# A fused attention and two expert layers on one core: conversions that keep a word in PSUM, pieces of 768 columns, one more shared buffer

## The chip, the core and the metric

The kernel runs on one core of a Trainium2 chip. The metric is the device time of one execution in microseconds, lower is better. The engines are TensorE (PE; its weight loads are listed as PEld), VectorE (DVE), ScalarE (ACT) and GpSimd (POOL). SyncE (SP) issues the DMA transfers.

## What is computed

```python
def _attn_ref(q, k, v, centroids):              # q, k, v: (2, 8, 768, 64)
    q_assign = np.argmax(np.einsum('bhsd,hcd->bhsc', q_n, c_n), axis=-1)
    k_assign = np.argmax(np.einsum('bhsd,hcd->bhsc', k_n, c_n), axis=-1)
...
    scores = np.where(mask, scale * q @ k.T, -1000000000.0)
    attn = np.exp(scores - np.max(scores, axis=-1, keepdims=True))
    attn = attn / (np.sum(attn, axis=-1, keepdims=True) + 1e-09)
    return np.matmul(attn, v)
...
def _moe_ref(x, w_in, w_out):                   # 1536 tokens, 512 -> 2048 -> 512
    h = x @ w_in
    return (h * np.cos(h)) @ w_out
...
def _moe2_ref(x, w_in, w_out):
    h = x @ w_in
    return (h * (1.0 / (1.0 + np.exp(-h)))) @ w_out
```

The code is condensed. A query sees only the keys of its own cluster (16 clusters for each head). The attention's result, 1536 tokens of 512 numbers, goes through the first expert layer and then the second. The four weight matrices come in with eight bytes for each number.

## The kernel before

**Numbers.** A product that must keep the accuracy of 32 bits is made of three passes of TensorE on 16-bit halves: high by high, high by low, low by high. So nearly every operand is split: a high half is a cast (mostly on ScalarE), a low half is the value less its high half (VectorE or GpSimd).

**Weights.** `conv` (L683) turns 512 columns of double-width numbers, loaded into a staging buffer, into 32-bit floats by integer operations on VectorE: L692 shifts the upper word and writes the target, L694 takes the sign and exponent from the upper word and joins them with what L692 wrote, in place, and the low word follows in one of two ways. Either VectorE joins it (L701), or, where the table `LOW` says so (2 of every 4), ScalarE makes a number of it (L698) and GpSimd adds it (L699). There are 64 such conversions: 16 for each of the two matrices of layer 1 (`w1_prep`, L782), 16 for the second matrix of layer 2 (`w2_convert`, L853; its result goes to DRAM and returns later), and 16 for the first matrix of layer 2 (`layer2`, L1101), after the attention's buffers have been given up. Then the weights are scaled and split: high half on ScalarE (L738) or GpSimd (L739), low half on VectorE (L750), on GpSimd, or by TensorE (`pe_lo`, L722).

**Attention** (L869). Seven units of one or two tiles of 128 queries, eight heads each: 96 tiles of 128 queries by 768 keys. Of each: scores on TensorE into a PSUM buffer (L890), the row maximum on VectorE (L900), scale and bias of the exponent (L904, L905; VectorE or GpSimd), the exponential on ScalarE into one of four buffers `e` (L919), the high half on ScalarE (L926) or VectorE (L928), the low half on GpSimd (L933) or VectorE (L935), a transposing DMA into a buffer of kind `pT` (L512), and the product with v on TensorE (L943). After eight heads VectorE makes x from the sums (L952 to L954, L960) and splits it (L967, L969, or ScalarE and GpSimd, L970), and a DMA transposes it.

**Layers.** `layer1_in` (L996) takes a unit's x through the first matrix in pieces of `EW` columns: TensorE into PSUM (L1019 to L1021), then L1034 (ScalarE), L1035 (VectorE), a sine (L1037), L1040 (VectorE), the high half (L1042, ScalarE) and the low half (L1043, GpSimd). `layer1_out` (L1049) makes the second product. `layer2` does the same in three passes of 512 tokens, once layer 1 is done: L1170 and L1172 split x, then pieces of `EW` columns (L1190 to L1206) and the second product (L1221 to L1223).

**Buffers.** PSUM has three tiles `pb` of 1024 columns, which hold scores, pieces of the layers, transposes on TensorE and the sums of the preparation, and two tiles of 512 (`g2_ps`, `xn_ps`). In SBUF there are four buffers `e` of `EW` columns and `NGEN` shared buffers `gen` of 768 columns, which serve four kinds; `LEAST` says how many are kept back for each kind (`pT` 3).

**What sets the order.** Each step is a task with a duration, a priority, its predecessors and the buffers that it takes. When the program is built, a list scheduler (`Graph.run`, L139) goes through the tasks in a model of time and takes on each engine the ready task of lowest priority number whose buffers are free; some tasks may go to either of two engines (`alt`), with a bias from the table. The priorities are sums of the entries of the table `T` (L22). What comes out is a fixed order for each engine. `port=True` marks tasks of VectorE that the model does not let run beside GpSimd.

Of the kernel before, what the change touches and what calls it, by code (L numbers as in the profile page):

```python
# [10 lines left out]
I32 = mybir.dt.int32  # L11
# [7 lines left out]
FG = 2.0 ** -19  # L19


T = dict(PW_IN=-2428, PW_OUT=-477, PW_STEP=783, W_AHEAD=-382, KV0=-981, KSTEP0=-32964, V0=33297, Q0=262, KSTEP=-17295,  # L22
         PREP=-1180, PREPQ=1313, LD=4990, LOB=-0.03, WB=-2.09, HB=1.22, EB=0.63, KB=-13.72, GB=2.92, CB=2.75, XB=1.77,
         SB=0.5, L2B=0.5, PV=-1944, HI=1053, LO=13021, XP=-1707, G1=1614, GE=-20317, GC=-1920, G2=1781, GO=-4433,
         W2=5268, XD=-9186, TB=2, WH=50.28, GATE=0)
UNITS = [(0, 0, 1), (0, 1, 1), (0, 2, 2), (0, 4, 2), (1, 0, 2), (1, 2, 2), (1, 4, 2)]

LOW = (2,2,2,2)

PRE = ((0,0),(1,0),(1,1),(0,1,0,1))  # L30

# [7 lines left out]

GRAM_XN = ()  # L40

EW = 1024
NE = 4
NGEN = 11

LEAST = {'stg':2,'natk':2,'ph':4,'pT':3}

WX, WXC = (0, 1), (1, 3)
EXP_BITS = 0x7F800000
# [185 lines left out]
def dve(cols, fast=False):  # L235
    return 0.069 + cols / (1920 if fast else 960)
# [10 lines left out]
def pool2(cols):  # L247
    return 0.15 + cols * 0.001887
# [21 lines left out]
def fused_kernel(tc, q, k, v, cent, w1i, w1o, w2i, w2o, out, dbg=None):  # L270
# [4 lines left out]
    P = 128  # L275
# [24 lines left out]
    with tc.manual_schedule(), tc.tile_pool(name="dram", bufs=1, space=DRAM) as dpool:  # L300
# [379 lines left out]
            xs_task[b] = add("DVE", 0.3, f, [sready[b, hp] for hp in range(NPAIR)], u * 1000)  # L680


        def conv(dst, acc, src, shape3, pri, dst_buf=None, pool=None, deps=(), dst_deps=(), add_low=False):  # L683

            w = Buf(pool or p_ws)
            wa = lambda: l2["ws"][w.ap] if isinstance(w.ap, int) else w.ap
            wi = lambda: wa().rearrange("p (a b) -> p a b", a=shape3) if shape3 else wa()
            word = lambda z: wa().rearrange("p (c two) -> p c two", two=2)[:, :, z]
            d = lambda: dst().bitcast(I32)
            l = add("SP", dma(P * WC * 8), lambda: SP.dma_start(out=wi(), in_=src), deps, pri - T["W_AHEAD"], acq=[w], lat=LLAT)  # L690
            ex = [dst_buf] if dst_buf else []
            a = add("DVE", dve(WC, True), lambda: DV.tensor_scalar(  # L692
                d(), word(1), 3, 0x3FFFFFFF, op0=ALU.logical_shift_left, op1=ALU.bitwise_and), [l, *dst_deps], pri, acq=ex, use=[w], port=True)
            b_ = add("DVE", dve(WC), lambda: DV.scalar_tensor_tensor(  # L694
                d(), word(1), -0x40000000, d(), op0=ALU.bitwise_and, op1=ALU.bitwise_or), [a], pri - 1, use=[w, *ex], port=True)
# [86 lines left out]
        def w1_prep():  # L782
# [41 lines left out]
            for d in range(ND):  # L824
# [276 lines left out]
        def layer2(l1_last):  # L1101
# [204 lines left out]
```

## Time and profile before

| | us |
|---|---|
| median of 3 executions | 826.79 (824.79 to 829.62) |
| the profiled execution | 824.2 |
| its span, from the first to the last instruction | 822.5 |
| TensorE busy, matmuls | 715.3 (87% of the span) |
| VectorE busy | 541.2 (66%) |
| ScalarE busy | 490.8 (60%) |
| GpSimd busy | 230.9 (28%) |
| mean granted TensorE clock | 0.958 of full speed |

The shares are means over the whole span, and the stages differ: the second expert layer, some 255 us at the end, has hardly any transfers and no GpSimd work, while the preparation of the weights and the attention lie in the first 460 us. A stage is therefore read by itself, in a table of windows, and the order of the work within it from a timeline of one engine. "Busy" leaves out waiting. The idle time in front of an instruction is put down to what ended it.

### The profile page before, as it was taken

How to read it: one execution, taken by the hardware profiler on the slowest of the kernel's cores; microseconds unless marked ns; L12 is line 12 of the kernel's file. 1: busy time of each engine (PE TensorE's matmuls, PEld its weight loads, DVE VectorE, ACT ScalarE, POOL GpSimd, SP SyncE). 2: the span in 40 equal slices, each digit the busy share in tenths (PEclk: the TensorE clock that was granted, in tenths of full speed). 3: DMA queues.
4: the chain of work that ended last, by engine and by line, in shares of the span. 5: the costliest groups of instructions: out<-in, count | busy, mean ns of one | idle time of the engine just before them, and what ended most of it. 6: DMA issues, size and time to landing. Idle time of an engine off the chain costs nothing.

```text
span 822.5 us, 16553 instructions
## 1 busy us (share of the span) xinstructions
PE 715.3 (87%) x6744; PEld 487.2 (59%) x6744; DVE 541.2 (66%) x1094; ACT 490.8 (60%) x702; POOL 230.9 (28%) x197
## 2 busy tenths in 40 slices
PE   2486677988779887899999999995999999999998
PEld 1353346777668765787787788882444444444443
DVE  7889988888789788989779756668670044004400
ACT  3769787888867766779659655548770045004400
POOL 3321634265452355346337323330000000000000
PEclk9967898999998999999999999997999999999999
DMA  8925799899999979978977986442312000000000
GB/s 273 358 71 160 196 196 189 148 167 187 177 183 195 248 146 174 176 194 176 183 163 127 214 183 216 141 132 75 104 51 77 26 1 0 26 26 1 0 26 26
DMA packets 233900, 111.27 MB, mean 135 GB/s; under 512 B 199520, under 2 KB 221536, under 8 KB 233824
## 3 DMA queue, kind: packets, MB, share of 16 engines
q1 hardware_dynamic: 233824, 110.23, 60.7%
q8 instruction: 52, 0.85, 0.4%
q14 instruction: 24, 0.20, 0.1%
HBM read 50.36 MB, written 10.49 MB: 74 GB/s over the span
## 4 chain that ended last, share of the span: by engine, by line
PE 58%; DVE 14%; DMA 13%; ACT 5%; issue 5%; POOL 2%; SPq 2%; POOLq 0%; DVEq 0%; ACTq 0%
DMA gen<-gen 7%; PE pb L1191 5%; PE pb L1192 5%; PE pb L1190 5%; PE pb L1019 4%; PE pb L1021 4%; PE pb L1020 4%; PE xn_ps L943 3%; PE pb L890 3%; DVE small L900 3%; PE xn_ps L1221 3%; PE g_ps L1221 3%; PE xn_ps L1223 3%; PE xn_ps L1222 3%; PE g_ps L1222 3%
## 5 line engine op out<-in xcount | busy, mean ns | idle before, releaser
L933 POOL TENSOR_TENSOR gen<-e,gen 128x768 f16<-128x768 f32 x67 | 110.0, 1656 | 63.4 <-ACT gen L926 47.3
L1078 PE MATMUL g_ps<-gT,w 128*128 128x256 f16 (+1 forms) x448 | 111.1, 260 | 3.3 <-POOL gT L1043 3.3
L919 ACT ACTIVATE e<-pb,small 128x768 f32<-128x768 f32 x96 | 94.7, 990 | 31.3 <-DVE small L905 11.9
L1019 PE MATMUL pb<-xT,w 128*128 128x256 f16 (+1 forms) x448 | 111.3, 260 | 1.8 <-DMA xT<-e 1.6
L1077 PE MATMUL g_ps<-gT,w 128*128 128x256 f16 (+1 forms) x448 | 111.2, 260 | 0.9 <-ACT x2s L1084 0.9
L1020 PE MATMUL pb<-xT,w 128*128 128x256 f16 (+1 forms) x448 | 111.2, 260 | 0.0
L1021 PE MATMUL pb<-xT,w 128*128 128x256 f16 (+1 forms) x448 | 111.2, 260 | 0.0
L1079 PE MATMUL g_ps<-gT,w 128*128 128x256 f16 (+1 forms) x448 | 111.2, 260 | 0.0
L900 DVE TENSOR_REDUCE small<-pb 128x1 f32<-128x768 f32 x96 | 89.3, 950 | 19.0 <-PE pb L890 17.0
L1202 DVE SCALAR_TENSOR_TENSOR e<-e,pb 128x1024 f32<-128x1024 f32 x24 | 29.3, 1219 | 105.2 <-ACT e L1200 105.1
L890 PE MATMUL pb<-kst,qst 96*128 96x512 f16 (+3 forms) x384 | 80.2, 343 | 18.0 <-ACT e L919 9.7
L943 PE MATMUL xn_ps<-vst,gen 128*128 128x64 f16 x1728 | 68.5, 196 | 21.5 <-DMA gen<-gen 19.8
L943 PEld LDWEIGHTS <-gen 128*128 128x128 f16 x1728 | 63.1, 100 | 33.5 <-DMA gen<-gen 26.4
L1190 PE MATMUL pb<-x2T,w 128*128 128x512 f16 x192 | 73.7, 384 | 4.5 <-ACT x2T L1170 4.5
L1043 POOL TENSOR_TENSOR gT<-e,gT 128x1024 f16<-128x1024 f32 x24 | 52.2, 2176 | 89.3 <-ACT gT L1042 80.4
L1191 PE MATMUL pb<-x2T,w 128*128 128x512 f16 x192 | 73.7, 384 | 2.5 <-DVE x2T L1172 2.5
L1192 PE MATMUL pb<-x2T,w 128*128 128x512 f16 x192 | 73.6, 383 | 0.0
L926 ACT ACTIVATE gen<-e 128x768 f16<-128x768 f32 x87 | 70.4, 840 | 2.1 <-DMA gen<-gen 0.9
L890 PEld LDWEIGHTS <-qst 128*128 128x128 f16 (+1 forms) x384 | 37.1, 101 | 41.7 <-issue 23.1
L1077 PEld LDWEIGHTS <-w 128*128 128x128 f16 x448 | 44.2, 99 | 9.8 <-issue 2.2
L1079 PEld LDWEIGHTS <-w 128*128 128x128 f16 x448 | 44.2, 99 | 7.8 <-issue 3.9
L1019 PEld LDWEIGHTS <-w 128*128 128x128 f16 x448 | 44.5, 99 | 5.6 <-DMA xT<-e 1.8
(201 smaller groups left out, 1515.0 us busy)
## 6 DMA issues: line engine op xcount, KB each, us to landing
ws<-in_moe_w_out_dram SPq DMA_DIRECT2D x24, 512.0 KB, 4.3
gT<-in_moe_w_in_dram SPq DMA_DIRECT2D x16, 512.0 KB, 5.7
ws<-in_moe_w_in_dram SPq DMA_DIRECT2D x16, 512.0 KB, 3.9
xT<-in_moe_w_out_dram SPq DMA_DIRECT2D x8, 512.0 KB, 4.8
w_dram<-x2s SPq DMA_DIRECT2D x16, 256.0 KB, 3.0
st<-w_dram SPq DMA_DIRECT2D x8, 512.0 KB, 4.4
gen<-in_k_dram SPq DMA_DIRECT2D x8, 384.0 KB, 6.7
gen<-in_v_dram SPq DMA_DIRECT2D x8, 384.0 KB, 5.2
```

The source lines that it names most:

```text
L890: PE.matmul(out=sbk.ap[:, c0:c1], lhsT=qs.ap[:kk, a, h], rhs=kb.ap[:kk, a, j].rearrange("p t c -> p (t c)")[:, c0:c1], start=(a == 1), sto ...
L900: DV.tensor_reduce(out=sm.ap[:, 0:1], in_=sbk.ap[:, :S], axis=AX.X, op=ALU.max, negate=True)
L943: PE.matmul(out=o, lhsT=hb.ap[:, pi, kt], rhs=vb.ap[:, vi, j, kt], start=(kt == 0 and pi == 0 and vi == 0), stop=(kt == NT - 1 and pi == 1 ...
L1019: PE.matmul(out=o, lhsT=wh[:, d, fs], rhs=xb.ap[:, 0, d, :n], start=(d == 0), stop=False)
L1020: PE.matmul(out=o, lhsT=wh[:, d, fs], rhs=xb.ap[:, 1, d, :n], start=False, stop=False)
L1021: PE.matmul(out=o, lhsT=wl[:, d, fs], rhs=xb.ap[:, 0, d, :n], start=False, stop=(d == ND - 1))
L1077: PE.matmul(out=o, lhsT=wh, rhs=gh, start=(f == 0 and i == 0), stop=False, skip_group_check=True)
L1078: PE.matmul(out=o, lhsT=wh, rhs=gl, start=False, stop=False, skip_group_check=True)
L1079: PE.matmul(out=o, lhsT=wl, rhs=gh, start=False, stop=(f == NF - 1), skip_group_check=True)
L1190: PE.matmul(out=o, lhsT=wh[:, d, fs], rhs=x[:, 0, d], start=(d == 0), stop=False)
L1191: PE.matmul(out=o, lhsT=wh[:, d, fs], rhs=x[:, 1, d], start=False, stop=False)
L1192: PE.matmul(out=o, lhsT=wl[:, d, fs], rhs=x[:, 0, d], start=False, stop=(d == ND - 1))
```

## The change

`conv` has a second form, chosen by the new table `VIA` for all conversions except those of `w2_convert`. In it the shift writes a PSUM buffer `pb` instead of the target. The mask reads that buffer; it writes the target where GpSimd adds the low word, and the PSUM buffer again where VectorE joins it, and then the low word's instruction reads PSUM and writes the target. The form has no `port=True`. `LOW` goes from (2,2,2,2) to (2,1,1,1), so that GpSimd adds the low word of 20 conversions instead of 32. `EW` goes from 1024 to 768, so that layer 1 works in pieces of 768 columns and layer 2, whose blocks are 512 wide, in pieces of 512. `NGEN` goes from 11 to 12 and the buffers kept back for `pT` from 3 to 4. All priorities of `T` are new.

```diff
-T = dict(PW_IN=-2428, PW_OUT=-477, PW_STEP=783, W_AHEAD=-382, KV0=-981, KSTEP0=-32964, V0=33297, Q0=262, KSTEP=-17295,
+T = dict(PW_IN=-24521, PW_OUT=-778, PW_STEP=537, W_AHEAD=-3139, KV0=502, KSTEP0=-8482, V0=2122, Q0=-1625, KSTEP=-1911,
...
-LOW = (2,2,2,2)
+LOW = (2,1,1,1)
+
+VIA = (4,4,0,4)
...
-EW = 1024
+EW = 768
 NE = 4
-NGEN = 11
-
-LEAST = {'stg':2,'natk':2,'ph':4,'pT':3}
+NGEN = 12
+
+LEAST = {'stg':2,'natk':2,'ph':4,'pT':4}
...
+            if via:
+
+                mb = Buf(p_pb)
+                m = lambda: mb.ap[:, :WC].bitcast(I32)
+                a = add("DVE", dve(WC), lambda: DV.tensor_scalar(
+                    m(), word(1), 3, 0x3FFFFFFF, op0=ALU.logical_shift_left, op1=ALU.bitwise_and), [l], pri, acq=[mb], use=[w])
+                to, td, tu = (d, dst_deps, ex) if add_low else (m, (), [])
+                b_ = add("DVE", dve(WC), lambda: DV.scalar_tensor_tensor(
+                    to(), word(1), -0x40000000, m(), op0=ALU.bitwise_and, op1=ALU.bitwise_or), [a, *td], pri - 1, acq=tu, use=[w, mb])
+            else:
...
             if add_low:
...
+            elif via:
+                c_ = add("DVE", dve(WC), lambda: DV.scalar_tensor_tensor(
+                    d(), word(0), 29, m(), op0=ALU.logical_shift_right, op1=ALU.bitwise_or), [b_, *dst_deps], pri - 2, acq=ex, use=[w, mb])
```

Over the whole program TensorE issues as many rows as before. VectorE's low halves of the attention (L935, 29) are gone and GpSimd has all 96. GpSimd has 25 scalings of weights (L739, none before), and ScalarE 15 instead of 40 (L738). In the rows below the new program's lines are L698 for the shift into PSUM, L701 for the mask, L713 for the low word from PSUM and L716 for the old form of it; the row maximum is L915, and L935, L933, L954, L969, L1035, L1040 and L1043 have become L950, L948, L969, L984, L1050, L1055 and L1058.

VectorE at the start of the program, where the first matrix of layer 1 is converted (`gT` holds the loaded words, `w_108` is the target, `e_116` the centroids). Before:

```order
L692 TENSOR_SCALAR w_108<-gT 128x512
L694 SCALAR_TENSOR_TENSOR w_108<-gT,w_108 128x512
L457 TENSOR_TENSOR e_116<-e_116 128x64
L458 TENSOR_REDUCE cols<-e_116 128x1
L459 TENSOR_SCALAR cols<-cols 128x1
L692 TENSOR_SCALAR w_108<-gT 128x512
L694 SCALAR_TENSOR_TENSOR w_108<-gT,w_108 128x512
L692 TENSOR_SCALAR w_108<-gT 128x512
```

and with the change:

```order
L698 TENSOR_SCALAR pb_64<-gT 128x512
L701 SCALAR_TENSOR_TENSOR w_108<-gT,pb_64 128x512
L698 TENSOR_SCALAR pb_68<-gT 128x512
L701 SCALAR_TENSOR_TENSOR w_108<-gT,pb_68 128x512
L698 TENSOR_SCALAR pb_72<-gT 128x512
L701 SCALAR_TENSOR_TENSOR pb_72<-gT,pb_72 128x512
L698 TENSOR_SCALAR pb_64<-gT 128x512
L713 SCALAR_TENSOR_TENSOR w_108<-gT,pb_72 128x512
L701 SCALAR_TENSOR_TENSOR pb_64<-gT,pb_64 128x512
```

The conversions now stand ahead of the centroids' first step, one after the other, with three `pb` buffers in turn.

VectorE behind the 64th row maximum, at the end of a tile's x (`small` are the softmax sums; `gen` a tile's two halves). Before:

```order
L969 TENSOR_TENSOR e_112<-e_112 128x512
L952 TENSOR_SCALAR small<-small 128x8
L953 RECIPROCAL small<-small 128x8
L954 TENSOR_TENSOR small<-small,cols 128x8
L935 TENSOR_TENSOR gen_216<-e_116,gen_216 128x768
L935 TENSOR_TENSOR gen_212<-e_124,gen_212 128x768
L935 TENSOR_TENSOR gen_220<-e_120,gen_220 128x768
L428 TENSOR_SCALAR dmax<-ident,cols 128x128
L1035 SCALAR_TENSOR_TENSOR e_116<-e_116,cols,pb_64 128x1024
L692 TENSOR_SCALAR x2s<-ws_244 128x512
L694 SCALAR_TENSOR_TENSOR x2s<-ws_244,x2s 128x512
L701 SCALAR_TENSOR_TENSOR x2s<-ws_244,x2s 128x512
```

and with the change:

```order
L984 TENSOR_TENSOR e_112<-e_112 128x512
L967 TENSOR_SCALAR small<-small 128x8
L968 RECIPROCAL small<-small 128x8
L969 TENSOR_TENSOR small<-small,cols 128x8
L503 SCALAR_TENSOR_TENSOR natq_236<-stq,cols,natq_236 128x8x64
L430 TENSOR_SCALAR dmax<-ident,cols 128x128
L716 SCALAR_TENSOR_TENSOR x2s<-ws_248,x2s 128x512
L1050 SCALAR_TENSOR_TENSOR e_124<-e_124,cols,pb_68 128x768
L1055 SCALAR_TENSOR_TENSOR e_124<-e_124,pb_68 128x768
```

The three low halves that stood between the sums and the piece of layer 1 are gone from VectorE, and the piece has 768 columns.

GpSimd where the pieces of layer 1 of the first unit with two tiles lie (`gT` takes the low half of a piece). Before:

```order
L699 TENSOR_TENSOR x2s<-x2s,ws_244 128x512
L933 TENSOR_TENSOR gen_192<-e_112,gen_192 128x768
L1043 TENSOR_TENSOR gT<-e_124,gT 128x1024
L1043 TENSOR_TENSOR gT<-e_120,gT 128x1024
L1043 TENSOR_TENSOR gT<-e_116,gT 128x1024
L970 TENSOR_TENSOR e_112<-e_112 128x512
L557 TENSOR_SCALAR natka<-ohb 128x12x16
```

and with the change:

```order
L559 TENSOR_SCALAR natq_236<-ohb 128x8x16
L948 TENSOR_TENSOR gen_188<-e_124,gen_188 128x768
L948 TENSOR_TENSOR gen_208<-e_112,gen_208 128x768
L1058 TENSOR_TENSOR gT<-e_116,gT 128x768
L1058 TENSOR_TENSOR gT<-e_124,gT 128x768
L1058 TENSOR_TENSOR gT<-e_112,gT 128x768
```

Two low halves of the attention stand ahead of the pieces, and the pieces are narrower and more in number.

## Rows read from the trace of the kernel before

**Rows 1.** Windows: stretch, length, busy us (instructions) of PE, PEld, DVE, ACT, POOL; clock, DMA share, GB/s.
```profile
0.00:66.90 66.90, 36.91 (x314) 24.91 (x315) 57.08 (x151) 40.98 (x50) 18.76 (x48) 0.90 0.68 232
66.90:128.20 61.30, 39.84 (x377) 23.24 (x376) 55.49 (x131) 52.84 (x85) 27.26 (x22) 0.81 0.78 182
128.20:337.20 209.00, 174.56 (x2481) 142.81 (x2479) 177.38 (x418) 154.94 (x244) 97.11 (x73) 0.95 1.00 180
337.20:460.10 122.90, 117.64 (x1446) 98.66 (x1446) 101.46 (x201) 96.25 (x150) 60.09 (x39) 1.00 0.91 173
460.10:557.00 96.90, 94.11 (x977) 83.84 (x976) 59.66 (x93) 52.78 (x85) 27.68 (x16) 1.00 0.64 175
557.00:568.00 11.00, 1.57 (x10) 0.69 (x8) 10.38 (x34) 8.83 (x11) 0.00 (x0) 0.73 0.08 25
568.00:822.50 254.50, 250.65 (x1151) 113.04 (x1150) 79.77 (x72) 84.22 (x82) 0.00 (x0) 0.99 0.10 34
```
**Rows 2.** Timeline of VectorE: start, us, engine, line; row maxima 1, 16 and 64.
```profile
66.93 0.95 DVE L900 TENSOR_REDUCE small<-pb 128x1 f32<-128x768 f32 x1
...
128.17 0.96 DVE L900 TENSOR_REDUCE small<-pb 128x1 f32<-128x768 f32 x1 [0.35 <-ACT gen L926]
...
337.22 0.95 DVE L900 TENSOR_REDUCE small<-pb 128x1 f32<-128x768 f32 x1
```
**Rows 3.** Waits: who, for whom, us in total, times, longest us.
```profile
PEld L943 <- DMA gen<-gen: 26.4, 26, 3.0
...
DVE small L900 <- PE pb L890: 17.0, 17, 2.3
```
**Rows 4.** Groups of VectorE by line: count, busy us, mean ns, idle us before them.
```profile
L1035 DVE SCALAR_TENSOR_TENSOR e<-e,cols,pb 128x1024 f32<-128x1024 int32 x24 | 30.7, 1278 | 23.6 <-ACT e L1034 23.4
L935 DVE TENSOR_TENSOR gen<-e,gen 128x768 f16<-128x768 f32 x29 | 29.0, 1021 | 1.3 <-ACT gen L926 1.3
L905 DVE TENSOR_SCALAR small<-small 128x1 f32<-128x1 f32 x89 | 19.1, 214 | 3.1
...
L694 DVE SCALAR_TENSOR_TENSOR x2s<-ws,x2s 128x512 int32<-128x512 int32 x16 | 11.0, 688 | 0.2
...
L969 DVE TENSOR_TENSOR e<-e 128x512 f16<-128x512 f32 x11 | 8.9, 808 | 0.0
L960 DVE TENSOR_TENSOR e<-xn_ps,small 128x512 f32<-128x512 f32 x12 | 8.2, 687 | 5.8 <-PE xn_ps L943 5.5 <-POOL gen L933 0.2
...
L692 DVE TENSOR_SCALAR x2s<-ws 128x512 int32<-128x512 int32 x16 | 6.7, 422 | 0.2
...
L967 DVE CAST e<-e 128x512 f16<-128x512 f32 x12 | 6.2, 512 | 0.0
```
**Rows 5.** Windows up to the 64th maximum: VectorE's L692, then L694, then L701 alone.
```profile
0.00:337.20 337.20, 19.86 (x38) 0.91 0.90 190
...
0.00:337.20 337.20, 29.94 (x38) 0.91 0.90 190
...
0.00:337.20 337.20, 12.51 (x18) 0.91 0.90 190
```
**Rows 6.** Timeline of ScalarE and VectorE at the join between the layers.
```profile
562.83 1.99 ACT L1170 ACTIVATE x2T<-xf,cols 128x2048 f16<-128x2048 f32 x1
...
565.56 2.35 DVE L1172 SCALAR_TENSOR_TENSOR x2T<-xf,cols,x2T 128x2048 f16<-128x2048 f32 x1
```
**Rows 7.** Groups of GpSimd by line: one scaling of 512 columns.
```profile
L504 POOL TENSOR_SCALAR stq<-stq,cols 128x512 f32<-128x512 f32 x1 | 0.7, 694 | 1.2 <-ACT natq L651 1.2
```
**Rows 8.** Single lines: shortest, median and longest ns, first and last start.
```profile
L935 DVE TENSOR_TENSOR gen<-e,gen x29: 942/951/2226, 91.9 to 470.2; 128x768 f16<-128x768 f32 x29
...
L933 POOL TENSOR_TENSOR gen<-e,gen x67: 1629/1642/2093, 87.8 to 458.3; 128x768 f16<-128x768 f32 x67
...
L969 DVE TENSOR_TENSOR e<-e x11: 672/683/2049, 127.1 to 484.7; 128x512 f16<-128x512 f32 x11
```
**Rows 9.** A window of 4 us, columns as in rows 1.
```profile
204.00:208.00 4.00, 4.00 (x84) 4.00 (x82) 2.31 (x4) 2.44 (x4) 1.16 (x2) 1.00 1.52 187
```

More of the change, by code (lines that the diff above doesn't have):

```diff
@@ L19 @@
 FG = 2.0 ** -19
-T = dict(PW_IN=-2428, PW_OUT=-477, PW_STEP=783, W_AHEAD=-382, KV0=-981, KSTEP0=-32964, V0=33297, Q0=262, KSTEP=-17295,
-         PREP=-1180, PREPQ=1313, LD=4990, LOB=-0.03, WB=-2.09, HB=1.22, EB=0.63, KB=-13.72, GB=2.92, CB=2.75, XB=1.77,
-         SB=0.5, L2B=0.5, PV=-1944, HI=1053, LO=13021, XP=-1707, G1=1614, GE=-20317, GC=-1920, G2=1781, GO=-4433,
-         W2=5268, XD=-9186, TB=2, WH=50.28, GATE=0)
+T = dict(PW_IN=-24521, PW_OUT=-778, PW_STEP=537, W_AHEAD=-3139, KV0=502, KSTEP0=-8482, V0=2122, Q0=-1625, KSTEP=-1911,
+         PREP=-1178, PREPQ=1263, LD=-18051, LOB=-0.79, WB=1, HB=1, EB=5, KB=-3.59, GB=1.71, CB=0.8, XB=-0.2, SB=0.71,
+         L2B=48.54, PV=-3557, HI=4611, LO=8289, XP=6298, G1=1935, GE=-6473, GC=-1560, G2=2171, GO=-986, W2=18407,
+         XD=17052, TB=9.99, WH=-0.94, GATE=0)
 UNITS = [(0, 0, 1), (0, 1, 1), (0, 2, 2), (0, 4, 2), (1, 0, 2), (1, 2, 2), (1, 4, 2)]
-LOW = (2,2,2,2)
+LOW = (2,1,1,1)
+VIA = (4,4,0,4)
 PRE = ((0,0),(1,0),(1,1),(0,1,0,1))
@@ L680, in x_scale, with conv @@
             xs_task[b] = add("DVE", 0.3, f, [sready[b, hp] for hp in range(NPAIR)], u * 1000)
-        def conv(dst, acc, src, shape3, pri, dst_buf=None, pool=None, deps=(), dst_deps=(), add_low=False):
+        def conv(dst, acc, src, shape3, pri, dst_buf=None, pool=None, deps=(), dst_deps=(), add_low=False, via=False):
             w = Buf(pool or p_ws)
@@ L691, in conv @@
             ex = [dst_buf] if dst_buf else []
[L692 to L695, printed above, removed]
+            if via:
[7 more added lines that the diff above has]
+            else:
+                a = add("DVE", dve(WC, True), lambda: DV.tensor_scalar(
+                    d(), word(1), 3, 0x3FFFFFFF, op0=ALU.logical_shift_left, op1=ALU.bitwise_and), [l, *dst_deps], pri, acq=ex, use=[w], port=True)
+                b_ = add("DVE", dve(WC), lambda: DV.scalar_tensor_tensor(
+                    d(), word(1), -0x40000000, d(), op0=ALU.bitwise_and, op1=ALU.bitwise_or), [a], pri - 1, use=[w, *ex], port=True)
             if add_low:
@@ L795, in w1_prep @@
                 pr = PW_IN + i * 25
-                c_ = conv(lambda r=r: r, None, w_in_src(w1i, i), 0, pr, None, p_wg, add_low=i % 4 < LOW[0])
+                c_ = conv(lambda r=r: r, None, w_in_src(w1i, i), 0, pr, None, p_wg, add_low=i % 4 < LOW[0], via=i % 4 < VIA[0])
                 in_conv.append(c_)
@@ L830, in w1_prep @@
                     r = lambda c=c, d=d: place[d](c)
-                    c_ = conv(r, None, w_out_src(w1o, d, c), WC // P, pr + c, None, p_wx if c in WXC else None, dst_deps=dd[d], add_low=c < LOW[1])
+                    c_ = conv(r, None, w_out_src(w1o, d, c), WC // P, pr + c, None, p_wx if c in WXC else None, dst_deps=dd[d], add_low=c < LOW[1], via=c < VIA[1])
                     if c in WXC:
@@ L857, in w2_convert @@
                 pr = 1e6 + i * 10
-                t, tq = conv(lambda fb=fb: fb.ap, w2_mx[:, i:i + 1], w2o[i * P:(i + 1) * P, :].bitcast(I32), 0, pr, fb, dst_deps=x_free if 2 in WX else (), add_low=i % 4 < LOW[2])
+                t, tq = conv(lambda fb=fb: fb.ap, w2_mx[:, i:i + 1], w2o[i * P:(i + 1) * P, :].bitcast(I32), 0, pr, fb, dst_deps=x_free if 2 in WX else (), add_low=i % 4 < LOW[2], via=i % 4 < VIA[2])
                 w2_done.append(tq)
@@ L1112, in layer2 @@
                 r = slice(i * WC, (i + 1) * WC)
-                ms += conv(lambda r=r: raw(r), mx0[:, i:i + 1], w_in_src(w2i, i), 0, base + i * 10 - T["W2"], None, p_ws2, [t_swap], add_low=i % 4 < LOW[3])
+                ms += conv(lambda r=r: raw(r), mx0[:, i:i + 1], w_in_src(w2i, i), 0, base + i * 10 - T["W2"], None, p_ws2, [t_swap], add_low=i % 4 < LOW[3], via=i % 4 < VIA[3])
             def f_scale(z, mx, deps, pr):
```

## Prediction

> **What bounds the kernel now.** I read the stages first, by a table of windows [rows 1]. Its edges are the 1st, 16th and 64th row maximum of the softmax on VectorE [rows 2], the 96th at 460.1 us and the end of the first expert layer. In the table the reader is to see where TensorE idles. From 337.2 to 557 us it is busy 117.64 of 122.90 and 94.11 of 96.90 us, and in the second layer 250.65 of 254.50: those stretches are TensorE's. Its idle time lies before: 51.5 us up to the 16th maximum, 34.4 from there to the 64th (209.00 less 174.56), and 9.4 at the join between the layers. In just these stretches VectorE is busy 112.57 of 128.20 us and 177.38 of 209.00, and those sums leave out the gaps of some 0.05 us between its short instructions. Second, the waits: VectorE's largest wait for TensorE in the attention is 17.0 us in 17 pieces, small beside 337 us [rows 3]. So up to the 64th maximum VectorE's list of work sets the pace, and TensorE's waits on transposed weights (26.4 us) [rows 3] are late fruits of it.
>
> Price the whole list that VectorE holds ahead of the 64th maximum, each instruction by the mean of its group in the trace, and it comes to 319.0 us; the 64th maximum begins at 337.2 us [rows 2]. One microsecond of list is thus 337.2/319.0 = 1.06 us of time. The sum below uses that.
>
> **The change, term by term, up to the 64th maximum on VectorE.** Counts are from the order before and after.
> - *Subtractions of the attention's low halves.* All 96 now go to GpSimd; 15 of the 29 that VectorE had stood ahead of the 64th maximum, 24 ahead of the 96th. 15 x 1.021 [rows 4] = -15.3.
> - *Conversions of the weights.* Before, 38 shifts, 38 masks and 18 low words stood ahead of the 64th maximum and took 19.86 + 29.94 + 12.51 = 62.3 us [rows 5]; by the group means, by which the whole list is priced, it is 60.1. Now 32 go through PSUM: 32 shifts, 32 masks, 20 low words. No row shows a shift into PSUM. It cannot beat 0.42, the undisturbed shift between SBUF buffers (L692 on x2s), and should not pass 0.75, what L1035 with its PSUM operand takes for 1024 columns, 1.278, less 512 columns at 0.96 per ns [rows 4]. I take 0.68, near L960, which handles 512 columns with one operand in PSUM in 0.687 [rows 4]. 84 x 0.68 = 57.1; 7 old ones at 0.42 + 0.69 and 4 low words at 0.69 (L692 and L694 on x2s) [rows 4] add 10.5: 67.6. So +7.5, of which the six more low words (24 for 18; GpSimd adds fewer of them now) are the most. At the ends of the bound: 32 x 0.26 = 8.3 us less, or 84 x 0.07 = 5.9 us more.
> - *Layer pieces of 768 columns.* 12 of each of two passes where 8 stood, with the same columns: 8 more fixed parts of 1.278 - 1.067 = 0.21 us at most (L1035) [rows 4] = +1.5.
> - *Casts and copies* that go to ScalarE (L967 6 to 2, L969 5 to 3, L524 2 to 0, and L600, L654, L928): -7.5, L967 at 0.512 and L969 at 0.808 [rows 4]. ScalarE takes some 7 us and loses more than that, since 28 of its scalings of weights go to GpSimd; it was busy 154.94 of 209.00 us [rows 1]. If it were the bound there, those 7 us would come back.
> - *Scale and bias of the exponent*, five pairs from GpSimd: 5 x 0.42 (L905 and its twin) [rows 4] = +2.1. The rest (two L498, one L501, small ones): +0.9.
>
> Sum: -10.8, or -11.4 us of time. It is not even. Ahead of the 16th maximum VectorE's list grows by 8.4 (the conversions and the splits are all pulled in front), from there to the 64th it shrinks by 19.2. TensorE must then pack the work of that stretch into about 189 us instead of 209; it holds 6 us less of work there, as that too moved ahead. 168/189 is 0.89 busy, where the next stretch shows 0.96 [rows 1], so there is room.
>
> From the 64th to the 96th maximum VectorE's list falls by another 9, which I count at nothing: TensorE covers it with 117.64 of 122.90 us; what could come back is at most those 5.3 us of idle time. After the 96th TensorE has the same matmuls left. **Join**: the second layer's first product waits for the low half of x2, which VectorE begins at 565.56 behind two weight splits and the scales, while ScalarE had finished the high half at 564.82 [rows 6]. Now one split and all three sets of scales stand ahead: 1.3 us less, 1.3 more. Nothing. Without that balance it is 2 us. **Second layer**: pieces of 512 columns double the instruction count on VectorE and ScalarE, hidden by 250.65 us of TensorE; a piece takes TensorE 2.6 us and its way through the others about the same, with three buffers. Were the cover gone at each of the three passes, some 2 us each. GpSimd's new scalings (0.694 us for 512 columns [rows 7]) lie beside VectorE and ScalarE, as GpSimd has 97.11 busy of 209.00 [rows 1]. SyncE's transposes keep their number; the twelfth shared buffer lets a fourth transposed tile wait for TensorE, which is worth nothing while VectorE is late.
>
> The profiled execution took 824.2 us; less 11.4 is 812.8. The median of the runs is 826.8, 2.6 above it, and the forecast for a median carries that: 815.4. Its own range is 804 (the idle 5.3 us and the cheap shift as well) to 822 (dear shift, join and second layer lose their 2 us each).
>
> Here the trace and two rules stand against each other. The same subtraction takes 951 ns on VectorE and 1642 on GpSimd, 1.73 times as long [rows 8]. The Trainium skill, GPSIMD Engine Reference, section Engine selection, says to keep elementwise work with two inputs on VectorE, as GpSimd is about twice as slow; the trace agrees on the ratio, and by the rule this move loses, which is the first rival. The other rule bears on what remains on VectorE. Its instructions on SBUF alone are at times stretched: L969 means 808 ns with an undisturbed 0.68 [rows 4, 8]. The Trainium skill, SBUF — State Buffer, section Who interferes with whom, says that a VectorE instruction with two SBUF inputs waits for a GpSimd instruction that reads SBUF, and that one with a single SBUF input does not; by it the conversions come free of such waits, while the others wait more as GpSimd works about a fifth more: an estimate of 1 to 3 us, or some 817.
>
> **Rivals.**
> 1. *GpSimd's subtraction sits in the path.* Each moved one takes 0.69 us longer, and if the probabilities' transposes, which wait for it, are what TensorE needs next, 15 x 0.69 = 10.4 us come back: 825.8. For: TensorE's waits on DMA, 26.4 us. Against: GpSimd is half idle there, and another buffer holds tiles ahead.
> 2. *PSUM runs short.* The three pb buffers also hold scores and transposes. 12 x 1.36 + 20 x 2.04 = 57 us of holding in the first 137 us. If each of 32 conversions delays something by 0.35 us, the gain is gone: the change doesn't do what it says, 826.8.
> 3. *The transfers bound the middle.* The DMA share is 1.00 from the 16th to the 64th maximum [rows 1]. If the stretch cannot shrink below 209 us, the late start stays: 826.8 + 8.4 = 835.2. Against: short windows show 1.52 [rows 9], and 209 us move at 180 GB/s, the opening at 232.
> 4. *The late start is not made up* (slower). Ahead of the first maximum VectorE's list grows from 66.1 to 88.6, so the attention starts 23 us later, with TensorE only 8 us further on. If the middle is held by latencies rather than by VectorE's list, 15 us are lost: 841.8. It decides itself at the 16th maximum: beyond 143 us this rival holds, near 137 mine.
>
> **How the numbers follow.** Forecast 0.60; rival 1 0.13; rival 2 0.07; rival 3 0.09; rival 4 0.11. A change of 0.5%, about what a measurement of this kernel can tell, is 4.1 us: below 822.7 is faster, above 830.9 slower. Faster 0.60, the same 0.20 (rivals 1 and 2), slower 0.20 (3 and 4). The range reaches from 804 to 835.5, which takes in rival 3 and leaves out rival 4 and a few hundredths below.
>
> **What would show it.** Right: the first maximum near 90 us, the 16th near 137, the 64th near 326, the 96th near 449; no SBUF subtraction on VectorE; conversions of 0.65 to 0.7 us without outliers; TensorE about 0.89 busy in the middle; the second layer 254 us long. Wrong: shifts into PSUM far over 0.75, waits of VectorE for a free pb, TensorE's waits on transposes grown by ten microseconds, or GpSimd over 0.8 busy.

## The result

The changed kernel takes 817.24 us (median of 4 executions, 815.30 to 818.29) against 827.27 us for the kernel before: a ratio of 0.9874, 95% interval 0.9846 to 0.9902, or 10.0 us less. In a later comparison, with other kernels beside it, it was 0.9893 (0.9851 to 0.9935). The profiled execution took 815.3 us, its span is 813.6. The forecast was 815.4, and the middle of the program behaved nearly as forecast. Several of the steps that led there are wrong all the same, as the experiments show.

Windows of the changed kernel, the columns as in [rows 1]; the edges are its own 1st, 16th, 64th and 96th row maximum and the first product of the second layer:

```profile
0.00:85.90 85.90, 46.31 (x381) 30.18 (x382) 74.83 (x195) 53.49 (x69) 25.78 (x57) 0.98 0.69 228
85.90:135.50 49.60, 35.03 (x410) 20.99 (x409) 43.71 (x104) 36.69 (x60) 31.37 (x26) 0.97 0.86 164
135.50:320.00 184.50, 160.38 (x2370) 133.83 (x2367) 162.68 (x398) 152.59 (x251) 108.48 (x77) 0.97 1.06 196
320.00:448.00 128.00, 121.18 (x1458) 100.59 (x1458) 101.31 (x199) 100.94 (x166) 72.61 (x49) 0.99 0.93 173
448.00:551.70 103.70, 94.85 (x983) 84.59 (x981) 70.90 (x124) 59.44 (x102) 35.65 (x25) 0.99 0.59 161
551.70:813.60 261.90, 251.56 (x1152) 113.19 (x1151) 94.21 (x128) 88.76 (x124) 14.12 (x8) 0.98 0.10 33
```

The first maximum comes 19 us later than before and the 16th 7 us later; from there to the 64th 184.4 us pass where 209.0 did, with TensorE 0.87 busy and the transfers at 196 GB/s instead of 180. The stretch to the 96th gives 5 us back (128.1 for 122.9), and so does the second layer (261.9, where 257.6 lay between its first product and the end before). The maxima by themselves, in VectorE's timeline (the answers to [rows 2]; the last is the 96th):

```profile
85.87 0.96 DVE L915 TENSOR_REDUCE small<-pb 128x1 f32<-128x768 f32 x1 [0.72 <-PE pb L905]
...
135.55 0.94 DVE L915 TENSOR_REDUCE small<-pb 128x1 f32<-128x768 f32 x1
...
319.96 0.95 DVE L915 TENSOR_REDUCE small<-pb 128x1 f32<-128x768 f32 x1
...
448.04 0.96 DVE L915 TENSOR_REDUCE small<-pb 128x1 f32<-128x768 f32 x1 [0.38 <-PE pb L905]
```

The conversions through PSUM, line by line (shortest, median and longest ns; 3 of the 14 groups): shifts with medians of 690 to 694 ns where 680 was assumed, and no long ones.

```profile
L698 DVE TENSOR_SCALAR pb<-ws x24: 676/694/722, 24.7 to 542.9; 128x512 int32<-128x512 int32 x24
...
L701 DVE SCALAR_TENSOR_TENSOR pb<-ws,pb x16: 679/690/720, 55.1 to 543.6; 128x512 int32<-128x512 int32 x16
...
L713 DVE SCALAR_TENSOR_TENSOR w<-ws,pb x13: 676/686/687, 102.9 to 544.4; 128x512 int32<-128x512 int32 x13
```

Of the waits that answer to [rows 3], TensorE's on transposed weights went from 26.4 to 28.9 us and VectorE's on scores from 17.0 to 11.0:

```profile
PEld L958 <- DMA gen<-gen: 28.9, 31, 2.1
...
DVE small L915 <- PE pb L905: 11.0, 16, 1.4
```

What is new stands at the join of the layers. Here is its timeline on GpSimd (POOL), VectorE, ScalarE (one line) and TensorE:

```profile
547.72 2.21 POOL L754 TENSOR_SCALAR w<-w,cols 128x1024 f16<-128x1024 f32 x2 [11.60 <-DVE dmax L430]
...
548.19 0.66 DVE L407 TENSOR_TENSOR cols<-cols 128x1 f32<-128x1 f32 x1
...
548.95 0.99 DVE L1180 TENSOR_TENSOR cols<-cols 128x1 f32<-128x1 f32 x1
...
549.67 1.99 ACT L1185 ACTIVATE x2T<-xf,cols 128x2048 f16<-128x2048 f32 x1
...
549.91 1.12 POOL L762 TENSOR_SCALAR w<-w,cols 128x1024 f32<-128x1024 f32 x1
...
550.05 0.99 DVE L1182 SCALAR_TENSOR_TENSOR cols<-cols 128x1 f32<-128x1 f32 x1
...
551.12 2.12 POOL L763 TENSOR_TENSOR w<-w 128x1024 f16<-128x1024 f32 x1
...
551.53 1.73 DVE L407 TENSOR_TENSOR cols<-cols 128x1 f32<-128x1 f32 x1
551.71 0.59 PE L1205 MATMUL pb<-x2T,w 128*128 128x512 f16 x1 [3.75 <-ACT x2T L1185]
...
554.59 0.16 DVE L407 TENSOR_TENSOR cols<-cols 128x1 f32<-128x1 f32 x1
...
556.38 2.34 DVE L1187 SCALAR_TENSOR_TENSOR x2T<-xf,cols,x2T 128x2048 f16<-128x2048 f32 x1
...
558.78 0.59 PE L1206 MATMUL pb<-x2T,w 128*128 128x512 f16 x1 [6.48 <-DVE x2T L1187]
```

An operation on one number per partition, 0.16 us by itself, takes 0.66, 0.99, 0.99 and 1.73 us on VectorE and ends with the GpSimd instruction beside it: 3.7 us more in the four. TensorE waits 6.48 us for the low half of x2 (L1187), where it had waited 2.51 at this place before:

```profile
567.96 0.59 PE L1191 MATMUL pb<-x2T,w 128*128 128x512 f16 x1 [2.51 <-DVE x2T L1172]
```

### The profile page after: what moved, and what is told of

Same layout as the page of the kernel before. It is cut to its first block, busy times and chain, and to the rows that moved or that the text cites. A ratio compares the mean times of both kernels' runs of the same rounds, so it can differ in the third digit from the quotient of the medians.

```text
span 813.6 us, 16849 instructions
## 1 busy us (share of the span) xinstructions
PE 709.3 (87%) x6744; PEld 483.4 (59%) x6744; DVE 547.6 (67%) x1143; ACT 491.9 (60%) x767; POOL 288.0 (35%) x239
## 4 chain that ended last, share of the span: by engine, by line
PE 41%; DVE 7%; DMA 5%; issue 2%; POOL 2%; ACT 2%; SPq 1%; POOLq 0%; DVEq 0%; ACTq 0%
PE pb L1206 5%; PE pb L1207 5%; PE pb L1205 5%; DMA gen<-gen 3%; PE xn_ps L1236 3%; PE xn_ps L1238 3%; PE g_ps L1236 3%; PE xn_ps L1237 3%; PE g_ps L1237 3%; PE g_ps L1238 3%; PE g_ps L1094 2%; PE g_ps L1093 2%; PE g_ps L1092 2%; DMA ws<-in_moe_w_in_dram 2%; POOL gen L948 1%
## 5 line engine op out<-in xcount | busy, mean ns | idle before, releaser
L948 POOL TENSOR_TENSOR gen<-e,gen 128x768 f16<-128x768 f32 x96 | 159.0, 1667 | 55.2 <-ACT gen L941 29.3
L1035 PE MATMUL pb<-xT,w 128*128 128x256 f16 (+1 forms) x448 | 111.0, 261 | 0.0
L915 DVE TENSOR_REDUCE small<-pb 128x1 f32<-128x768 f32 x96 | 89.7, 951 | 11.7 <-PE pb L905 11.0
L1217 DVE SCALAR_TENSOR_TENSOR e<-e,pb 128x512 f32<-128x512 f32 x48 | 32.7, 685 | 95.9 <-ACT e L1215 95.9
L1058 POOL TENSOR_TENSOR gT<-e,gT 128x768 f16<-128x768 f32 (+2 forms) x36 | 56.0, 1559 | 93.3 <-ACT gT L1057 86.2
L958 PE MATMUL xn_ps<-vst,gen 128*128 128x64 f16 x1728 | 66.3, 195 | 21.5 <-DMA gen<-gen 20.6
L958 PEld LDWEIGHTS <-gen 128*128 128x128 f16 x1728 | 60.2, 99 | 34.2 <-DMA gen<-gen 28.9
L941 ACT ACTIVATE gen<-e 128x768 f16<-128x768 f32 x89 | 73.1, 841 | 0.2
L1221 DVE SCALAR_TENSOR_TENSOR w<-e,w 128x512 f16<-128x512 f32 x48 | 33.8, 708 | 24.6 <-ACT w L1219 24.3
L1215 ACT ACTIVATE e<-pb,cols 128x512 f32<-128x512 f32 x48 | 32.9, 684 | 28.1 <-PE pb L1207 28.1
L1092 PEld LDWEIGHTS <-w 128*128 128x128 f16 x448 | 44.1, 98 | 9.0 <-issue 0.6
```

Source lines behind the costliest of these rows:

```text
L948: tl = add("POOL", pool2(S), lambda hi=hi, lo=lo, ex=ex: PO.tensor_tensor(lo(), ex(), hi(), op=ALU.subtract), [th], pr + T["LO"], use=[*eu ...
L958: PE.matmul(out=o, lhsT=hb.ap[:, pi, kt], rhs=vb.ap[:, vi, j, kt], start=(kt == 0 and pi == 0 and vi == 0), stop=(kt == NT - 1 and pi == 1 ...
L1035: PE.matmul(out=o, lhsT=wh[:, d, fs], rhs=xb.ap[:, 1, d, :n], start=False, stop=False)
L1092: PE.matmul(out=o, lhsT=wh, rhs=gh, start=(f == 0 and i == 0), stop=False, skip_group_check=True)
```

## The experiments

Each changes the one or the other kernel in one respect, or in two or three that the text names. "Own order" means that the order on each engine stays as it was, but for what the diff shows. Where a kernel was planned anew, its scheduler made a new order. The table gives the stages as lengths in us of the profiled executions (their edges as above, from the timelines), and the ratio of the times to the kernel before. A maximum that is computed twice counts once. The changed kernel stands twice in the table: its stages differ by 1 to 2 us from one execution to the next, so a smaller difference in a stage says nothing. The profiled execution of e2 (822.5 us) is among the shortest of its ten, those of e6 (830.7) and e11 (828.9) are the longest of theirs.

| | to 16th | to 64th | to 96th | to layer 2 | layer 2 | ratio (95%) |
|---|---|---|---|---|---|---|
| before | 128.2 | 209.0 | 122.9 | 104.8 | 257.6 | 1 |
| changed | 135.5 | 184.4 | 128.1 | 103.7 | 261.9 | 0.987 (0.985 to 0.990) |
| changed, once more (e5) | 134.6 | 182.3 | 129.2 | 104.0 | 260.9 | 0.989 (0.985 to 0.994) |
| e1 maxima doubled | 138.5 | 189.5 | 128.1 | 104.6 | 260.8 | 0.998 (0.995 to 1.000) |
| e2 GpSimd doubled | 135.2 | 190.4 | 128.9 | 104.5 | 261.7 | 1.002 (0.999 to 1.005) |
| e3 ScalarE doubled | 134.9 | 187.1 | 129.0 | 105.3 | 261.9 | 0.996 (0.993 to 0.998) |
| e4 words in SBUF | 154.2 | 183.2 | 129.9 | 112.4 | 261.7 | 1.020 (1.017 to 1.024) |
| e6 before, subtractions moved | 128.9 | 213.6 | 124.6 | 104.4 | 257.2 | 1.004 (1.001 to 1.006) |
| e7 subtractions moved back | 134.2 | 186.6 | 129.8 | 105.9 | 261.1 | 0.992 (0.989 to 0.995) |
| e8 join | 134.4 | 183.5 | 129.1 | 103.5 | 257.8 | 0.986 (0.981 to 0.990) |
| e9 before, PSUM alone | 137.2 | 211.8 | 124.3 | 103.4 | 266.7 | 1.024 (1.018 to 1.030) |
| e10 before, order alone | 147.3 | 199.4 | 128.9 | 101.8 | 261.1 | 1.015 (1.010 to 1.020) |
| e11 1024 columns, 11 buffers | 138.6 | 192.1 | 129.5 | 106.5 | 260.5 | 1.001 (0.999 to 1.004) |
| e12 no PSUM, planned anew | 148.1 | 193.7 | 128.1 | 105.5 | 261.1 | 1.017 (1.012 to 1.022) |

**Which engine paces.** e1, e2 and e3 do sixteen instructions of one engine twice, in the changed kernel's own order, one for every fourth of the first 64 tiles: the row maximum, the subtraction, the cast of the high half. The edit of e1:

```diff
-                    def f_m(sbk=sbk, sm=sm):
-                        DV.tensor_reduce(out=sm.ap[:, 0:1], in_=sbk.ap[:, :S], axis=AX.X, op=ALU.max, negate=True)
+                    def f_m(sbk=sbk, sm=sm, twice=h % 4 == 0 and u < 5):
+                        for _ in range(2 if twice else 1):
+                            DV.tensor_reduce(out=sm.ap[:, 0:1], in_=sbk.ap[:, :S], axis=AX.X, op=ALU.max, negate=True)
```

> The changed kernel in its own order, but VectorE computes the row maximum twice for 16 of the first 64 tiles of 128 queries by 768 keys (every fourth head): 16 x 0.95 = 15.2 us more on VectorE's list ahead of the 64th maximum, and nothing else. Theory (VectorE's list sets the pace up to the 64th maximum): the 64th maximum moves from 320 us by 15 to 16 us, the time from 817 to 831 to 834. Rival (TensorE, the transfers or latencies hold the middle in the changed kernel): the 64th maximum moves by less than 6 us and the time stays under 824.

> The changed kernel in its own order, but GpSimd makes the subtraction of the low half twice for the same 16 tiles: 16 x 1.64 = 26 us more on GpSimd ahead of the 64th maximum. Theory (GpSimd lies beside, 108 of 184 us busy between the 16th and the 64th maximum): less than 5 us, time 817 to 822. Rival (the subtraction sits in the path to the transposes): 10 us or more, over 827.

> The changed kernel in its own order, but ScalarE makes the cast of the high half twice for those of the same 16 tiles whose cast it makes: up to 16 x 0.84 = 13.4 us more on ScalarE ahead of the 64th maximum, where it is busy 153 of 184 us. Theory (VectorE paces): less than 5 us, time up to 822. Rival (ScalarE has become the bound, as it took over casts): 10 us or more, over 827.

Measured: medians of 823.42, 828.18 and 820.86 us, the kernel before at 825.02 beside them. Against the changed kernel's 0.987 that is about 8 us for 15.2 us of VectorE, 12 for 26 of GpSimd and 7 for 13.4 of ScalarE (against its later 0.989 about 7, 11 and 5; their intervals reach some 3 us to either side). On each of the three a microsecond costs about half of one. The theory of a list that costs 1.06 for 1 falls, since e1 was to take 831 to 834 us, and so does "GpSimd lies beside". ScalarE's 820.86 lies within what the theory allowed. That the three engines hold the stretch together fits these costs but is not shown. In e2 VectorE is busy 558.7 us where the changed kernel has 547.6, without one instruction more, so part of GpSimd's price may be VectorE's waiting. In e1 TensorE is busy 252.9 us up to the 64th maximum, where the changed kernel has 241.7, at a granted clock of 0.94 for 0.97; so a part of that price may be slower matmuls. The first lines of the pages of the changed kernel and of e2:

```profile
PE 709.3 (87%) x6744; PEld 483.4 (59%) x6744; DVE 547.6 (67%) x1143; ACT 491.9 (60%) x767; POOL 288.0 (35%) x239
```

```profile
PE 710.9 (87%) x6744; PEld 484.2 (59%) x6744; DVE 558.7 (68%) x1143; ACT 493.6 (60%) x767; POOL 315.3 (38%) x255
```

**The subtractions.** e6 takes the kernel before in its own order and moves VectorE's 29 subtractions to GpSimd; e7 takes the changed kernel and moves 16 back.

```diff
-                                 alt=("DVE", dve(S), lambda hi=hi, lo=lo, ex=ex: DV.tensor_tensor(lo(), ex(), hi(), op=ALU.subtract), T["EB"]))
+                                 alt=("DVE", dve(S), lambda hi=hi, lo=lo, ex=ex: PO.tensor_tensor(lo(), ex(), hi(), op=ALU.subtract), T["EB"]))
```

> The kernel before in its own order, but the 29 subtractions of the attention's low halves that stood on VectorE go to GpSimd at the same places. Nothing else changes. Theory of the prediction (VectorE's list alone paces, 1.06 us for each): 15.3 us less ahead of the 64th maximum, time 808 to 813. Rival (several engines hold the stretch together, as the doubled instructions suggest, some 0.5 us for each us of VectorE and 0.4 for each of GpSimd's; and conversions in SBUF suffer from more work on GpSimd): 15.3 x 0.5 less and 25 x 0.4 more, time 822 to 832.

> The changed kernel in its own order, but 16 of the 64 subtractions ahead of the 64th maximum (every fourth head) go back from GpSimd to VectorE at the same places. Theory of the prediction (VectorE's list alone paces): 16 x 0.95 = 15.2 us more, time 831 or more. Rival (what VectorE loses GpSimd wins, at some 0.5 and 0.4 us for each): within 5 us of the changed kernel.

> The changed kernel once more, unchanged, as the measure for the runs beside it: 0.985 to 0.990 of the kernel before.

Measured: e6 828.23 us (1.004 of before), e7 818.65, and 816.93 for the changed kernel beside it. Where the step had -15.3, the move gains nothing in either kernel, as both rivals had it. The pages' busy times show what became of VectorE's gain. Kernel e6, then e7, the first line of each page:

```profile
PE 720.7 (87%) x6744; PEld 489.8 (59%) x6744; DVE 534.4 (64%) x1065; ACT 490.6 (59%) x702; POOL 280.6 (34%) x226
```

```profile
PE 710.8 (87%) x6744; PEld 484.9 (59%) x6744; DVE 549.2 (67%) x1159; ACT 491.7 (60%) x767; POOL 264.4 (32%) x223
```

VectorE was busy 541.2 us before and is 534.4 in e6, though 29.0 us of subtractions [rows 4] were taken from it: 22 us came back. Compared one by one, its other 1065 instructions are 19 us longer in e6. Up to the 64th maximum, where the step was counted, VectorE is busy 288.9 us for 290.0. In e7 it is the same with the other sign: 16 more subtractions, and 549.2 for 547.6. Even so the profiled e6 reaches the 64th maximum 5 us later (342.5 for 337.2). Some of that may be chance, as it is the longest execution of e6; the longer way through GpSimd, the first rival of the prediction, remains possible and was not tried by itself. The longer ones are found line by line; two groups of e6, whose shifts take 0.42 us when nothing disturbs them:

```profile
L692 DVE TENSOR_SCALAR gT<-ws x6: 418/788/1881, 55.4 to 130.2; 128x512 int32<-128x512 int32 x6
L692 DVE TENSOR_SCALAR gT<-xT x6: 412/964/1868, 55.7 to 131.3; 128x512 int32<-128x512 int32 x6
```

**The conversions.** e4 takes the changed kernel in its own order and lets the 48 conversions work in SBUF. The shift and the mask are issued where the first write of the target stood, so they come somewhat later than in the changed kernel. e12 leaves the PSUM form out and plans anew.

```diff
+                def f_sh():
+                    DV.tensor_scalar(d(), word(1), 3, 0x3FFFFFFF, op0=ALU.logical_shift_left, op1=ALU.bitwise_and)
+                    DV.scalar_tensor_tensor(d(), word(1), -0x40000000, d(), op0=ALU.bitwise_and, op1=ALU.bitwise_or)
```

```diff
-VIA = (4,4,0,4)
+VIA = (0,0,0,0)
```

> The changed kernel in its own order, but all 48 conversions that keep their middle word in PSUM write it to the target in SBUF, as before (shift and mask stand where the mask, or the low word, stood). No GpSimd or ScalarE instruction changes. Theory (only the list counts): undisturbed the shift takes 0.42 instead of 0.69 us; with the group means of before, 0.51 and 0.755, a conversion is 0.12 us shorter, so the 32 ahead of the 64th maximum save some 4 us: 813, the PSUM form by itself costs a little. Rival (the PSUM form is what keeps VectorE free of GpSimd's port): shifts and masks are stretched by the more work on GpSimd, means of over 0.6 and 0.85, and the time rises by 5 us or more, over 822.

> The changed kernel with all conversions in SBUF, planned anew, so that the planner keeps GpSimd's work clear of them in its model; priorities, low words, widths and buffers as changed. Theory (the PSUM form is the gain, also against an order that is planned without it): 830 or more. Rival (the 24 us of the fixed order were an order that did not fit): 821 or less.

Measured: 841.55 us (1.020) and 837.52 (1.017), some 24 and 20 us above the changed kernel's 817.24. By the time both are as the rival of e4 and the theory of e12 had it (over 822, 830 or more); of the rival's two means only the mask's is met. Ahead of the 64th maximum e4's 32 shifts take 17.27 us and its 32 masks 32.72 by VectorE's windows, a mean of 0.54 (the rival had over 0.6) and 1.02 (over 0.85). Most conversions take what they always took, and some three times as long. Of e4, line by line:

```profile
L699 DVE TENSOR_SCALAR w<-ws x18: 415/426/1868, 106.9 to 569.3; 128x512 int32<-128x512 int32 x18
...
L700 DVE SCALAR_TENSOR_TENSOR w<-ws,w x18: 691/693/2018, 107.5 to 569.7; 128x512 int32<-128x512 int32 x18
...
L715 DVE SCALAR_TENSOR_TENSOR w<-ws,w x13: 691/693/2097, 117.2 to 570.5; 128x512 int32<-128x512 int32 x13
```

One of them in e4's timeline, beside GpSimd's low half of a piece:

```profile
531.37 1.64 POOL L1060 TENSOR_TENSOR gT<-e,gT 128x768 f16<-128x768 f32 x1 [8.65 <-ACT gT L1059]
...
531.46 2.10 DVE L715 SCALAR_TENSOR_TENSOR w<-ws,w 128x512 int32<-128x512 int32 x1
```

GpSimd begins 0.09 us earlier and keeps its usual time; VectorE's 0.69 us become 2.10, which ends 0.55 us after GpSimd. So the instruction is not slowed, it waits. Of the 128 instructions of these conversions 26 take over 0.8 us in e4 and none in the changed kernel (the longest is 0.73), though 62 of its 128 begin while a GpSimd instruction runs. All 26 began while a GpSimd instruction ran, and ended at one and the same distance behind its end: 0.54 to 0.56 us for masks and low words, 0.28 or 0.29 for shifts. The conversions of `w2_convert`, which keep the old form in the changed kernel too, still have long ones there (L716, the low word: median 0.69, longest 2.14 us). VectorE's busy time on the page goes from 547.6 to 570.7 us.

The same can be added up for all of VectorE: what its instructions take beyond the median of their operation and shape, counted where it is over 0.2 us. Each instruction so counted up to the 64th maximum ran beside a GpSimd instruction and ended within its own usual time of that one's end. The sums up to there are 32.8 us before, 19.3 with the change (21.2 in e5), 41.7 in e4, 44.1 in e6 and 15.1 in e9 below; ahead of the 16th maximum alone they are 10.6, 3.1, 24.5, 14.7 and 2.6.

The cost of e4 falls where the conversions lie: 18.7 us ahead of the 16th maximum, 8.7 behind the 96th, none in the middle. How much of e4's loss is the later issue of the shifts was not tried by itself; e12, whose order was planned for SBUF with the changed kernel's priorities, loses about as much, 12.6 us of it ahead of the 16th maximum. A plan for SBUF with priorities of its own is the kernel before: against that one the change as a whole gains 10 us, not 24.

The Trainium skill, SBUF — State Buffer, section Who interferes with whom, says that VectorE and GpSimd share one pair of ports as an exclusive lock, that two SBUF inputs or a fast two-port mode make a VectorE instruction need it, and that one with at most one SBUF input outside those modes does not. The traces agree: the mask with two SBUF inputs (2.02 us) and the 0.42 us shift (1.87) get held in e4, and the same steps with a PSUM operand never. That the shift runs in a two-port mode is not in the trace; its 0.42 us against 0.69 into PSUM speaks for a faster mode.

**Parts of the change alone.** e9 puts the PSUM form into the kernel before, e10 the new priorities, and e11 takes the wide pieces and the eleven buffers back.

```diff
-EW = 768
+EW = 1024
-NGEN = 12
+NGEN = 11
-LEAST = {'stg':2,'natk':2,'ph':4,'pT':4}
+LEAST = {'stg':2,'natk':2,'ph':4,'pT':3}
```

> The kernel before with the PSUM form of the conversions alone (all but those of the matrix that goes to DRAM); priorities, low words, widths and buffers as before; the order is planned anew, as three buffers in PSUM are now taken by it. Theory after the runs so far (the PSUM form is what gains, as it does not hold VectorE and GpSimd apart): 812 to 821. Rival (the gain needs the new order as well, or PSUM runs short): 824 or more.

> The kernel before with the new table of priorities alone; conversions in SBUF, low words, widths and buffers as before. Theory (the conversions pulled to the front need the PSUM form): 830 or more, with the late start of the changed kernel and stretched conversions. Rival (the order by itself is the gain): 821 or less.

> The changed kernel with pieces of 1024 columns, 11 shared buffers and 3 kept for transposed tiles, as before; the rest as changed, the order planned anew. Theory (widths and the twelfth buffer are worth little beside the PSUM form): within 5 us of the changed kernel. Rival (the buffer lets TensorE run ahead): 824 or more.

Measured: 845.29 us (1.024), 836.28 (1.015) and 825.51 (1.001). Neither the PSUM form nor the order gains alone. e9 misses the 812 to 821 that I expected by over 20 us, although VectorE's waiting is the least of all in it (15.1 us by the sum above): less of it is not by itself less time. The table shows how form and order need each other. The order by itself does shorten the middle (199.4 for 209.0) and pays 19 us in front; with the PSUM form the front costs 7. The 12 us between the two fit VectorE's waits there, by the sum above 15.4 us in e10 and 3.1 in the changed kernel; e10 lacks the other parts of the change as well. For e9 the scheduler, with the old priorities, made the front 9 us and the second layer 9 us longer; what in that plan does it was not followed up. e11 misses my 5 us and comes out as its rival had it: the width and the buffer together are worth about 10 (0.987 or 0.989 against 1.001), most of it in the middle; which of the two, and how much is only the new plan, stays open.

**The join.** e8 is the changed kernel up to the second layer, where GpSimd splits no weights and the scales of the later passes wait for the first low half. It changes both at once; the diff shows the second.

```diff
-                ts = add("DVE", 1.17, f_s, [t, *t_scs], pr)
+                ts = add("DVE", 1.17, f_s, [t, *t_scs, *first], pr)
...
+                first = first or [tx]
```

> The changed kernel in its own order up to the second layer; there GpSimd takes no part in the splitting of the weights (ScalarE and VectorE do it), and the scales of the second and third pass are made behind the low half of the first x2 instead of ahead of it. Theory (the join was lengthened by GpSimd's scalings that hold VectorE's short instructions, and by three sets of scales ahead of the low half): the low half starts within 1 us of the end of the high half, TensorE's wait of 6.5 us for it shrinks to 2 or 3, time 4 us below the changed kernel. Rival (the second layer is longer because of its pieces of 512 columns): no change, within 1.5 us.

Measured: 811.84 us against 816.93 for the changed kernel on the same chip, 5.1 less; 0.986 of before (0.981 to 0.990). The intervals of the two ratios overlap; what shows the gain is the stage. The second layer is back at 257.8 us, where the changed kernel took 261.9 and 260.9, with pieces of 512 columns, so the rival falls. e11 says the same from the other side: with pieces of 1024 columns its second layer still takes 260.5. How much is GpSimd's scalings and how much the later scales was not parted. In e8's timeline the low half begins with the end of the high half, where it had begun 4.7 us behind it (556.38 for 551.66), and TensorE's wait is 1.80 us:

```profile
550.38 2.35 DVE L1193 SCALAR_TENSOR_TENSOR x2T<-xf,cols,x2T 128x2048 f16<-128x2048 f32 x1 [0.24 <-ACT x2T L1191]
...
552.78 0.59 PE L1213 MATMUL pb<-x2T,w 128*128 128x512 f16 x1 [1.80 <-DVE x2T L1193]
```

By its median it is the fastest of all kernels here.

## Why the prediction was right, and where its steps were wrong

- *The course in time* came out: maxima forecast near 90, 137, 326 and 449 us, measured at 85.9, 135.6, 320.0 and 448.0. That the late start is made up in the middle was right, and with it the sign and the size (11.4 us forecast, 10.0 measured). The middle won 24.6 us instead of 20, and what it won beyond the forecast paid for about half of what two stages lost that were counted at nothing (5.2 and 4.3 us).
- *The price of a conversion through PSUM* was right: 84 instructions at 0.68 were to make 57.1 us, and the 32 + 32 + 20 of them take 22.01 + 21.93 + 13.58 = 57.5 by VectorE's windows.
- *"15 x 1.021 = -15.3" for the subtractions* is wrong. The runs put nothing in its place (e6, e7). It priced what leaves VectorE and left out that each one on GpSimd makes what is left wait longer. The second rule, weighed at "1 to 3 us", came to some 20 us in e6. The first rival (a longer way through GpSimd) is not excluded: e2's 12 us and the later 64th maximum of e6 fit it too. The second rule as the prediction gave it frees every VectorE instruction with a single SBUF input, and that is too wide: the shift of 0.42 us has one such input and was held (1.87 us in e4). The condition that it leaves out, on the two-port modes, is told above with the conversions.
- *"+7.5" for the conversions* compares with the wrong thing. The old means were those of a GpSimd with less to do. With the new order and the new load the old form costs 24 us more than the new one (e4; 20 in e12). The term that looked like a small loss is, in this order, what keeps the gain.
- *The two errors cancel in the sum.* VectorE's busy time up to the 64th maximum fell from 290.0 us [rows 1] to 281.2 (74.83 + 43.71 + 162.68), 8.7 less where the list had 10.8, and VectorE's waits for GpSimd fell from 32.8 to 19.3 us, though GpSimd was busy 288.0 us for 230.9: its longer work meets fewer instructions that it can hold. The forecast counted on neither. That its sum came out so close is in part luck: the course in time was understood, two of its largest terms were not.
- *"One microsecond of list is 1.06 us of time"* is wrong for the changed kernel: about half (e1), and as much on GpSimd and ScalarE (e2, e3). The 319.0 us of the list were durations that overlap each other: VectorE was busy 290.0 of the 337.2 us [rows 1], so 47 us lay idle and 1.06 did not measure how tightly it paces. The kernel before was not doubled, so what a microsecond costs there stays open.
- *TensorE's clock* was no term of the sum. Up to the 64th maximum TensorE was busy 251.3 us before [rows 1] and 241.7 with the change, for nearly the same matmuls (3172 and 3161 in the rows). The granted clock, a mean of its two levels of 1.2 and 2.4 GHz, rose from 0.81 to 0.97 between the 1st and the 16th maximum (0.87 in e5, where TensorE was busy 243.8 us in all) and from 0.95 to 0.97 from there to the 64th. How much of the 10 us that gave was not tried, nor what raised it; the prediction's sum cannot tell, as it counts VectorE alone.
- *The middle* was forecast at 189 us with TensorE 0.89 busy: 184.4 and 0.87. Rival 3 (the transfers bound it) falls: they moved 196 GB/s at a share of 1.06.
- *Rival 2* (PSUM runs short) falls for the changed kernel: shifts into PSUM waited for a free buffer once, 0.3 us, and TensorE's waits up to the 64th maximum that a conversion in a `pb` buffer ended come to 7.1 us in 8 pieces, not 11.
- *The stretch to the 96th maximum*, counted at nothing, became 5 us longer. No run tells why.
- *"Join: Nothing"* is wrong by 4.3 us. The instructions were counted, 1.3 less and 1.3 more, but not the GpSimd scalings that the order put beside them, which held four of VectorE's for 3.7 us altogether. e8 gets it back.
- *"Worth nothing" for the twelfth buffer and "+1.5" for the width*: together about 10 us of gain, if e11's new plan is a fair measure.
- *Rival 4* had its own test, the 16th maximum beyond 143 us, and a price of 841.8. The changed kernel stays below. e4, e10 and e12 lie beyond, at 147 to 154, and take 836 to 842 us: without the PSUM form its test and its price would have been met, but not its mechanism, since the middle of e4 is as short as with the change (183.2) and the loss lies in front.

## What to carry to other kernels

Before moving an instruction from VectorE to GpSimd, look at what VectorE will run beside it: a group of instructions whose median is normal and whose longest is three times as long was held here, and the held time grew with GpSimd's load (32.8 to 44.1 us in e6). A single operand kept in PSUM was dearer by the row (0.69 for 0.42 us) and, in this order, cheaper by 24 us. Parts of a change that was planned as a whole need not have a sign of their own; try each alone, and the whole without it.

## What was not expected of the hardware

A VectorE instruction on 128 numbers can take 1.73 us instead of 0.16 while GpSimd works on a large tile beside it, and ends with it. And taking 29.0 us of work from VectorE lowered its busy time by only 6.8.
